# All attention in native float32 products on halves of the array, and another order for the first two chunks

## The chip, the cores and the metric

The kernel runs on one core of one Trainium2 chip. The metric is the device time of one execution in microseconds (us). Before the change the median of three runs is 740.6 us (740.05, 740.6, 743.92).

## The reference

Attention with a local window and a few global columns, and behind it a two-layer network with a GELU, all in float32:

```python
scores = q @ k.T / sqrt(64) - slope[h] * dist          # dist = i - j, or n_local for far global columns
scores = where(is_global | is_local, scores, -1e9)     # n_global = 8 columns, n_local = 96 rows back
a = exp(scores - max) / (sum + 1e-9)
x = a @ v                                              # 4 batches, 8 heads, 768 tokens, 64 per head
h = x.reshape(3072, 512) @ w_in                        # 512 -> 2048
out = gelu(h) @ w_out                                  # 2048 -> 512
```

The weights arrive as float64 words and are turned into float32 on the chip.

## The kernel before, in words

**Tiles.** The 3072 tokens are cut into 12 chunks of 256 (three per batch); a chunk is two blocks of 128 queries. Each block looks at 256 columns: its own 128, the 96 before them and the 32 that hold the global ones (the first block of a batch needs 128). The eight heads of a chunk form four pairs. The network is cut into 8 slices of 256 hidden units. A step `t` is one (chunk, slice), 96 in all: `m1` (line 480) makes `h` with 24 products of 256 columns, `gelu` (495) turns it into `gh + gl`, `m2` (506) adds 12 products of 512 columns to the accumulators `acc`. x, the weights and g are each held as a float32r part and a remainder ("hi" and "lo"), so that three float32r products stand for one of full precision.

**Attention before.** Chunks 0 and 1 (`NATIVE`) multiply plain float32: `scores_pair` (314) puts the two heads of a pair on rows 0-63 and 64-127 of the array, `av_pair` (459) puts them on columns 0-63 and 64-127. The profile shows every such product as two instructions. All other chunks use `split_qk`, `split_v`, `scores` (345), `av_mm` (424): q, k, v and the flipped probabilities are cut into hi and lo by GpSimd, VectorE and ScalarE, and each head then takes whole-array float32r products, 4 per head for the scores (`s`, line 367), 4 for the values (`av`, line 443; 3 in the first chunk of a batch). In both forms VectorE adds the bias and takes the minimum (`n`, `mn`), ScalarE makes the exponentials, GpSimd normalises `n` (line 398), PE transposes it (`t`, line 411) and ScalarE copies it out (`pt`).

**Weights.** Words of a slice come in four pieces of 512 KB (`w`, line 156) through four buffers; `split_weights` (167) decodes a piece: ScalarE the low word, VectorE three operations, ScalarE hi, VectorE lo (lines 180 to 195). Slice s is decoded at step `DECODE[s]` = -6, -4, ..., 8.

**Order.** `run` (561) walks T from -11 to 95 and records m1 of step T+1, m2 of step T and whatever attention falls due: chunk c starts at `START[c]`, and `EV`/`EVN` give the offsets of its parts. `STEPS` starts with slices 0 and 1 of chunk 0, then of chunk 1; from slice 2 on the two chunks take turns. A scheduler then places each engine's instructions by its own estimate of when they become ready; each engine runs its own list in that order. The DMAs of the kernel are issued by SP, q of chunk 0 and the outputs by ScalarE's queue.

Of the kernel before, what the change touches and what calls it, by code (L numbers as in the profile page):

```python
# [17 lines left out]
P = 128  # L18
# [18 lines left out]
EV = {"split": (-1, 0, 3, 4), "v": (3, 4, 7, 8), "s": (0, 1, 4, 5), "exp": (2, 6),  # L37
      "pt": (4, 5, 8, 9), "av": (4, 5, 8, 9)}
EVN = {"split": (-1, 0, 1, 1), "v": (-1, 0, 2, 2), "s": (0, 1, 2, 3), "exp": (0, 1, 3, 3),
       "pt": (2, 3, 4, 5), "av": (2, 3, 4, 5)}  # L40

DECODE = (-6, -4, -2, 0, 2, 4, 6, 8)
LATE = 5

V_POOL = (2,)
NEGMASK = -1000000000.0
WARM_S = False
# [6 lines left out]
def load_scalars(nc, pool, src, name):  # L54
    w = pool.tile([P, 2, 2], I32, name=name + "_w")
    nc.scalar.dma_start(w.rearrange("p i t -> p (i t)"), src.bitcast(I32).partition_broadcast(P))
    f = pool.tile([P, 2, 2], F32, name=name + "_f")
# [12 lines left out]
class Fast:  # L70
    def __init__(self, tc, ctx, qT, kT, v, w, out, limits):
# [10 lines left out]
        self.kq = pool("kq", 2)  # L82
        self.vp = pool("vp", 2)
        self.pp = pool("pp", 4)
# [10 lines left out]
        self.pt_n, self.pt_t, self.av, self.x = {}, {}, {}, {}  # L95
        self.stat, self.g, self.h = {}, {}, {}
        self.acc, self.t3 = {}, {}
        self.last_table = self.last_word = self.last_hi = None

    def consts(self):  # L100
        nc, const = self.nc, self.const
        self.nl, self.ng = load_scalars(nc, const, self.limits, "nn")
        self.ident = const.tile([P, P], F32, name="ident")
        make_identity(nc, self.ident)
        self.pen = const.tile([P, 2 * P], BF16, name="pen")
        self.pen0 = const.tile([P, P], BF16, name="pen0")
        self.kg = const.tile([P, H, 2, NG], F32, name="kg")
        self.nmax = const.tile([P, 8], F32, name="nmax")
        nc.vector.memset(self.nmax, NEGMASK)
        self.qsc = const.tile([P, NP], F32, name="qsc")  # L110
        for p in range(NP):
            for hh in range(2):
                nc.gpsimd.memset(self.qsc[hh * D:(hh + 1) * D, p:p + 1], 1.0 / (8.0 * slope(2 * p + hh)))
        self.wand = const.tile([P, 256], I32, name="wand")
        nc.vector.memset(self.wand, -1)
        ta = self.stg.tile([P, 4, 256], F32, name="ta", tag="stage")
        tb = self.stg.tile([P, 4, 256], F32, name="tb", tag="stage")
        irel, icol = tb[:, 0].bitcast(I32), tb[:, 1, 0:P].bitcast(I32)
        rel, col, keep = ta[:, 0], ta[:, 1, 0:P], ta[:, 2]
        nc.gpsimd.iota(irel, pattern=[[-1, 2 * P]], base=P, channel_multiplier=1)  # L120
        nc.gpsimd.iota(icol, pattern=[[1, P]], base=0, channel_multiplier=0)
        nc.vector.tensor_copy(rel, irel)
        nc.vector.tensor_copy(col, icol)
        nc.vector.tensor_scalar(out=col, in0=col, scalar1=self.ng, scalar2=None, op0=ALU.is_lt)
        nc.vector.tensor_scalar(out=col, in0=col, scalar1=BIG, scalar2=-BIG, op0=ALU.mult, op1=ALU.add)
        nc.vector.tensor_scalar(out=col, in0=col, scalar1=self.nl, scalar2=None, op0=ALU.subtract)
        nc.vector.tensor_scalar(out=keep, in0=rel, scalar1=self.nl, scalar2=None, op0=ALU.is_lt)
        nc.vector.scalar_tensor_tensor(out=keep, in0=rel, scalar=0.0, in1=keep, op0=ALU.is_ge, op1=ALU.mult)
        nc.vector.tensor_scalar(out=keep, in0=keep, scalar1=BIG, scalar2=-BIG, op0=ALU.mult, op1=ALU.add)
        nc.vector.tensor_tensor(out=self.pen, in0=keep, in1=rel, op=ALU.subtract)  # L130
# [3 lines left out]
    def after(self, ins, prev, why):  # L134
        self.tc.add_manual_dep(
            ins, prev.name, mybir.DependencyInfo(mybir.DependencyClass.NoSync, mybir.DependencyReason.DATA),
            reason=why)

# [11 lines left out]
    def lo_dve(self, out, in_, hi):  # L150
        self.nc.vector.tensor_tensor(out=out, in0=in_, in1=hi.bitcast(F32), op=ALU.subtract)  # L151

    def load_words(self, s, i, use):
# [3 lines left out]
        if use == "w":  # L157
            if self.last_word is not None:
                self.after(ins, self.last_word, "weights in order")
            self.last_word = ins  # L160
        return w

    def load_weights(self, s):
        for i in range(4):
            self.raw[s, i, "w"] = self.load_words(s, i, "w")

    def split_weights(self, s):
        nc = self.nc
        if s == LATE:
            self.early.close()  # L170
            self.wts = self.ctx.enter_context(self.tc.tile_pool(name="wlate", bufs=1, side="right"))
        if s == NST - 1:
            self.words.close()
            self.wts = self.ctx.enter_context(self.tc.tile_pool(name="wlast", bufs=1))
        for nm, dst, shape in (("win", self.win, [P, 4, 256]), ("wout", self.wout, [P, 2, 512])):
            dst[s] = tuple(self.wts.tile(shape, F32R, name=f"{nm}{k}{s}") for k in "hl")
        for i in range(4):
            w = self.raw.pop((s, i, "w"))
            lw, hw = w[:, :, 0], w[:, :, 1]
            ins = nc.scalar.activation(out=lw, in_=lw.bitcast(U32), func=AF.Copy, scale=2.0 ** -29).ins  # L180
            if self.last_hi is not None:
                self.after(ins, self.last_hi, "a piece begins when ScalarE is through with the one before")
            a = self.sm.tile([P, 512], I32, name=f"wb{s}_{i}", tag="o")
            nc.vector.tensor_scalar(out=a, in0=hw, scalar1=0x07FFFFFF, scalar2=3,
                                    op0=ALU.bitwise_and, op1=ALU.logical_shift_left)
            nc.vector.scalar_tensor_tensor(out=a, in0=hw, scalar=-0x40000000, in1=a,
                                           op0=ALU.bitwise_and, op1=ALU.bitwise_or)
            nc.vector.tensor_tensor(out=a, in0=a, in1=lw, op=ALU.add)  # L188
            af = a.bitcast(F32)
            if i < 2:  # L190
                hi, lo = (x[:, 2 * i:2 * i + 2, :].rearrange("p d f -> p (d f)") for x in self.win[s])
            else:
                hi, lo = (x[:, i - 2, :] for x in self.wout[s])
            self.last_hi = nc.scalar.copy(hi, af).ins
            self.lo_dve(lo, af, hi)
# [4 lines left out]
    def check_words(self, n):  # L200
# [3 lines left out]
        for e in range(2):  # L204
            nc.vector.scalar_tensor_tensor(out=self.wand, in0=w[:, e * 256:(e + 1) * 256, 1], scalar=0x40000000,
                                           in1=self.wand, op0=ALU.bitwise_xor, op1=ALU.bitwise_and)

    def load_glob(self, b):
        self.kgr = self.stg.tile([P, H, NG], F32, name=f"kgr{b}", tag="stage", padded_shape=[P, H, 128])
        for u in range(2):  # L210
            self.nc.sync.dma_start(self.kgr[u * D:(u + 1) * D], dap(self.kT, b * H * D * S, [[S, D], [D * S, H], [1, NG]]))

    def split_glob(self):
        self.hi_pool(self.kg[:, :, 0, :].bitcast(F32R), self.kgr)
        self.nc.vector.tensor_tensor(out=self.kg[:, :, 1, :], in0=self.kgr, in1=self.kg[:, :, 0, :], op=ALU.subtract)

    def load_qk(self, c, p):
        nc = self.nc
        b, cc = divmod(c, CPB)
        k0 = (b * H + 2 * p) * D * S  # L220
        first = cc == 0
        nb = 1 if first else 2
        if c in NATIVE:
            kr = self.es.tile([P, nb, 256], F32, name=f"kr{c}_{p}", tag="kn", bufs=4)
            qr = self.es.tile([P, CT], F32, name=f"qr{c}_{p}", tag="qn", bufs=4)
            if first:
                nc.sync.dma_start(kr[:, 0, :], dap(self.kT, k0, [[S, P], [1, 256]]))
            else:
                nc.sync.dma_start(kr[:, :, NG:256], dap(self.kT, k0 + cc * CT - 96, [[S, P], [P, 2], [1, 224]]))
                nc.sync.dma_start(kr[:, :, 0:NG], dap(self.kT, k0, [[S, P], [0, 2], [1, NG]]))  # L230
            (nc.scalar if c == 0 else nc.sync).dma_start(qr, dap(self.qT, k0 + cc * CT, [[S, P], [1, CT]]))
            self.raw[c, p] = (kr, qr, nb)
            return
        if p == 0 and (cc == 1 or c == len(NATIVE)):
            self.load_glob(b)
# [572 lines left out]
```

## Time and profile before

| | |
|---|---|
| profiled execution, own time | 742.26 us |
| its span in the trace | 740.5 us |
| median of the runs shown | 740.6 us |
| PE busy | 701.2 us (95%) |
| VectorE busy | 500.8 us (68%) |
| ScalarE busy | 355.7 us (48%) |
| GpSimd busy | 324.9 us (44%) |
| DMA | 80.92 MB, mean 109 GB/s |

Matmuls overlap each other, so the time that a product costs the stream is read from the distance of two starts, not from its duration. "Granted clock" is the share of TensorE's full clock in a stretch.

### The profile page before, as it was taken

Reading aid. Unit: us, or ns where it says so; the run is one execution under the profiler, and the core shown is the slowest. Engines: PE = TensorE matmul, PEld = TensorE weight load, DVE = VectorE, ACT = ScalarE, POOL = GpSimd, SP = SyncE. Lnnn points to the kernel's source line nnn. Section 1 sums busy time; section 2 is a strip of 40 time slices with the busy share of each in tenths; the row PEclk is TensorE's granted clock in tenths of the full one; section 3 lists DMA queues with packets and bytes.
Section 4 is the critical chain, followed back from the end, with each engine's and each line's share of the span. In section 5 each row is a group of like instructions: output and inputs, shape, how many; then the busy total and the mean of one; then the engine's idle time right before and its main releaser. Section 6 shows DMA issues by size and latency. Waiting matters only on the chain.

```text
span 740.5 us, 13471 instructions
## 1 busy us (share of the span) xinstructions
PE 701.2 (95%) x4615; PEld 629.6 (85%) x4615; DVE 500.8 (68%) x1310; ACT 355.7 (48%) x906; POOL 324.9 (44%) x604
## 2 busy tenths in 40 slices
PE   4688998899999999999999999999999999999996
PEld 3446997788999999999889999999899999989995
DVE  6888898956856867866757857856658768634210
ACT  3567547356355455355355355354455455452101
POOL 3764135555345455443543554643444644431110
PEclk8558999999999999999999999999999999999999
DMA  8995552315334434334424334235334431100000
GB/s 247 244 242 184 159 168 73 112 52 158 109 94 122 129 104 115 100 93 126 110 94 135 113 109 128 87 101 128 104 104 119 129 111 43 44 15 1 30 1 32
DMA packets 74396, 80.92 MB, mean 109 GB/s; under 512 B 12368, under 2 KB 63056, under 8 KB 74320
## 3 DMA queue, kind: packets, MB, share of 16 engines
q1 hardware_dynamic: 70144, 73.16, 35.4%
q10 hardware_dynamic: 4176, 6.82, 2.6%
q8 instruction: 38, 0.62, 0.4%
q14 instruction: 38, 0.31, 0.1%
HBM read 73.66 MB, written 6.29 MB: 108 GB/s over the span
## 4 chain that ended last, share of the span: by engine, by line
PE 72%; DMA 10%; DVE 7%; ACT 4%; POOL 3%; issue 2%; SPq 1%; ACTq 0%; POOLq 0%; DVEq 0%
PE h L491 29%; PE acc L521 29%; PE av L443 4%; PE s L367 4%; PE t L411 4%; DMA c<-w 3%; POOL n L398 2%; DMA vr<-v 2%; ACT n L387 2%; DMA w<-w 2%; DMA kr<-kT 1%; DMA qr<-qT 1%; DVE wb L188 1%; DVE gl L151 1%; DVE n L372 1%
## 5 line engine op out<-in xcount | busy, mean ns | idle before, releaser
L491 PE MATMUL h<-xh,winh 128*128 128x256 f32 x768 | 219.1, 285 | 0.0
L491 PE MATMUL h<-xl,winh 128*128 128x256 f32 x768 | 218.0, 284 | 0.0
L491 PE MATMUL h<-xh,winl 128*128 128x256 f32 x768 | 216.7, 282 | 0.0
L521 PE MATMUL acc<-wouth,gh 128*128 128x512 f32 x384 | 154.0, 401 | 6.1 <-POOL gh L145 6.1
L521 PE MATMUL acc<-woutl,gh 128*128 128x512 f32 x384 | 151.6, 395 | 0.0
L491 PEld LDWEIGHTS h<-xh,winh 128*128 128x128 f32 x768 | 146.4, 191 | 2.8 <-issue 0.5
L491 PEld LDWEIGHTS h<-xl,winh 128*128 128x128 f32 x768 | 146.4, 191 | 2.0
L491 PEld LDWEIGHTS h<-xh,winl 128*128 128x128 f32 x768 | 146.3, 191 | 0.4
L398 POOL TENSOR_SCALAR n<-n,su 128x256 f32<-128x256 f32 (+1 forms) x192 | 100.9, 545 | 103.9 <-DVE su L392 89.9
L521 PE MATMUL acc<-wouth,gl 128*128 128x512 f32 x384 | 143.7, 397 | 2.0 <-DVE gl L151 2.0
L501 ACT ACTIVATE gr<-h 128x512 f32<-128x512 f32 x96 | 57.5, 599 | 152.6 <-PE h L491 104.2
L151 DVE TENSOR_TENSOR gl<-gr,gh 128x512 fp32r<-128x512 f32 x96 | 68.1, 710 | 91.1 <-POOL gh L145 91.1
L145 POOL TENSOR_SCALAR gh<-gr 128x512 fp32r<-128x512 f32 x96 | 64.1, 668 | 92.7 <-ACT gr L501 92.7
L145 POOL TENSOR_SCALAR vt<-vr 128x256 fp32r<-128x256 f32 (+1 forms) x80 | 34.5, 432 | 144.9 <-PE av L443 63.4
L387 ACT ACTIVATE n<-n,mn 128x256 f32<-128x256 f32 (+1 forms) x192 | 91.7, 480 | 6.2 <-DVE mn L336 6.0
L521 PEld LDWEIGHTS acc<-wouth,gl 128*128 128x128 f32 x384 | 72.6, 189 | 18.6 <-DVE gl L151 3.4
L521 PEld LDWEIGHTS acc<-wouth,gh 128*128 128x128 f32 x384 | 72.6, 189 | 18.4 <-POOL gh L145 7.5
L521 PEld LDWEIGHTS acc<-woutl,gh 128*128 128x128 f32 x384 | 72.7, 189 | 12.5
L411 PE MATMUL t<-ident,n 128*128 128x128 f32 x352 | 60.8, 291 | 18.0 <-POOL n L398 17.5
L450 ACT COPY t<-av 64x256 f32<-64x256 f32 x80 | 29.3, 366 | 98.2 <-PE av L443 94.7
L420 ACT CAST pt<-t 128x512 fp32r<-128x512 f32 (+1 forms) x80 | 44.3, 554 | 64.0 <-PE t L411 59.4
L411 PEld LDWEIGHTS t<-ident,n 128*128 128x128 f32 x352 | 42.4, 148 | 26.2 <-POOL n L398 22.7
(89 smaller groups left out, 1048.7 us busy)
## 6 DMA issues: line engine op xcount, KB each, us to landing
w<-w SPq DMA_DIRECT2D x32, 512.0 KB, 4.4
c<-w SPq DMA_DIRECT2D x32, 512.0 KB, 3.8
kr<-kT SPq DMA_DIRECT2D x112, 112.0 KB, 2.7
qr<-qT SPq DMA_DIRECT2D x84, 128.0 KB, 3.2
vr<-v SPq DMA_DIRECT2D x48, 128.0 KB, 2.3
out<-o ACTq DMA_DIRECT2D x24, 256.0 KB, 2.3
kr<-kT SPq DMA_DIRECT2D x28, 128.0 KB, 2.7
vr<-v SPq DMA_DIRECT2D x32, 96.0 KB, 2.2
```

Source lines behind the costliest of these rows:

```text
L145: self.nc.gpsimd.tensor_scalar(out=out, in0=in_, scalar1=scale, scalar2=0.0, op0=ALU.mult, op1=ALU.add)
L151: self.nc.vector.tensor_tensor(out=out, in0=in_, in1=hi.bitcast(F32), op=ALU.subtract)
L367: nc.tensor.matmul(sp[:, j, :w], lhsT=qq[:, hh, j * P:(j + 1) * P], rhs=kt[:, t, 0 if first else j, :w], start=t == 0, stop=t == 1)
L387: ins = nc.scalar.activation(out=nn[:, j, :w], in_=nn[:, j, :w], func=AF.Exp, bias=mn[:, i:i + 1], scale=-1.0, accum_out=su[:, i:i + 1])
L398: nc.gpsimd.tensor_scalar(out=nn[:, j, :w], in0=nn[:, j, :w], scalar1=su[:, i:i + 1], scalar2=0.0, op0=ALU.mult, op1=ALU.add)
L411: nc.tensor.transpose(tp[:, i, :], nn[:, j, a * P:(a + 1) * P], self.ident)
L420: nc.scalar.copy(pt[:, :, 0, :], tp[:, :n, :])
L443: nc.tensor.matmul(av[:, j], lhsT=vt[:, vi], rhs=pt[:, i], start=start, stop=stop)
L450: nc.scalar.copy(t1[hr], av[lr, :, 0, :])
L491: nc.tensor.matmul(hp[:, f, :], lhsT=w[:, d, f * P:(f + 1) * P], rhs=x[:, d, :], start=n == 0, stop=n == 3 * NP - 1)
L501: self.table(nc.scalar.activation(out=gr, in_=hp, func=AF.Gelu))
L521: nc.tensor.matmul(acc, lhsT=g[:, f, ks], rhs=w[:, f, :], start=s == 0 and n == 0, stop=s == NST - 1 and n == 5)
```

## The change

Every chunk now uses `scores_pair` and `av_pair`, and the splitting of q, k, v and of the probabilities, the copies of the global columns and the recombination `t1`, `t3` fall away (`split_qk`, `split_v`, `scores`, `av_mm`, `load_glob`, `split_glob`). GpSimd scales q by `qsc` and normalises, nothing else of the attention. A pair's parts follow each other by one step (`EVS`), its exponentials right behind its scores, so there are four batches of exponentials per chunk where there were two. Chunks 0 and 1 are attended first (`EVF`). The steps alternate between chunk 0 and chunk 1 from slice 0 on; two pieces are decoded per step, tied behind the reductions and the exponentials of earlier steps; two pieces may be in ScalarE's and VectorE's hands at a time. Loads of chunk 2 are tied behind slice 1. The constants are built in another order. The cores of the diff:

```diff
-NATIVE = (0, 1)
-START = [-10, -6, 4] + [8 * c - 13 for c in range(3, NCH)]
-STEPS = [(0, 0), (0, 1), (1, 0), (1, 1)] + [(c, s) for s in range(2, NST) for c in range(2)]
+START = [-9, -5] + [8 * c - 12 for c in range(2, NCH)]
+EVF = {"load": (-9, -9, -9, -9), "split": (-1, 0, 1, 2), "s": (0, 1, 2, 3), "pt": (1, 2, 3, 4), "av": (1, 2, 3, 4)}
+EVS = {"load": (-4, -2, 0, 2), "split": (-1, 1, 3, 5), "s": (0, 2, 4, 6), "pt": (1, 3, 5, 7), "av": (2, 4, 6, 8)}
+STEPS = [(c, s) for s in range(NST) for c in range(2)]
...
-DECODE = (-6, -4, -2, 0, 2, 4, 6, 8)
+DECODE = {(0, i): i - 4 for i in range(4)}
+DECODE.update({(s, i): 2 * s - 3 + i // 2 for s in range(1, NST) for i in range(4)})
...
-            if self.last_hi is not None:
-                self.after(ins, self.last_hi, "a piece begins when ScalarE is through with the one before")
+        if len(self.his) > 1:
+            self.after(ins, self.his[-2], "a piece begins when ScalarE is through with the last but one")
+        if self.last_table is not None:
+            self.after(ins, self.last_table, "a piece comes behind the exponentials of earlier steps")
...
+    def load(self, c, p):
...
+        def sync(out, in_):
+            ins = nc.sync.dma_start(out, in_)
+            if c == 2:
+                self.after(ins.ins, self.word_ins[1, 3], "behind the first slices")
+            return ins
...
+    def split(self, c, p):
+        kr, qr, vr = self.raw.pop((c, p))
+        self.hi_pool(qr, qr, self.qsc[:, p:p + 1])
...
-        self.warm(self.bank([P, 512], "warm_ps"), 14)
+        self.warm(self.bank([P, 512], "warm_ps"), 12)
+        self.limit_words = load_words2(self.nc, self.const, self.limits, "nn")
...
+        for p in range(NP):
+            self.load(1, p)
+            self.load_weights(0, p)
+        for s in range(1, NST - 1):
+            for i in range(4):
+                self.load_weights(s, i)
```

How the instructions stand now, at three places. Names carry chunk, head or pair, and a buffer number: s5_0 is the score bank of chunk 5, head 0; qr1_2 is q of chunk 1, pair 2; w1_3 is piece 3 of slice 1; h28 and gh28 belong to step 28.

**PE, between m1 and m2 of a step in the middle** (chunk 5's first scores). Before:

```order
L491 MATMUL h28_3244<-xh3_2196,winl4_928 128x256
L367 MATMUL s5_0_3285<-k5_0_3216,q5_0_3215 128x256 x4
L411 MATMUL t4_5_3293<-ident_129,n4_5_2942 128x128 x4
L521 MATMUL acc3_0_3060<-wouth3_809,gh27_3193 128x512
L521 MATMUL acc3_0_3060<-woutl3_810,gh27_3193 128x512
```

And now:

```order
L352 MATMUL h29_2921<-xh3_1942,winl5_1270 128x256
L270 MATMUL s5_0_2954<-kr5_0_2612,qr5_0_2613 128x256
L270 MATMUL s5_1_2955<-kr5_0_2612,qr5_0_2613 128x256
L270 MATMUL s5_0_2954<-kr5_0_2612,qr5_0_2613 128x256
L270 MATMUL s5_1_2955<-kr5_0_2612,qr5_0_2613 128x256
L382 MATMUL acc3_0_2666<-wouth4_1092,gh28_2883 128x512
```

One head's whole-array products (4 rows in one) have become the half-array products of two heads, enclosed by whole-array products on both sides; the values (`av`) stand likewise between m2 and m1.

**GpSimd, while chunk 0 is attended.** Before, the normalisations of pairs 0 and 1 (heads 0 to 3) followed each other:

```order
L398 TENSOR_SCALAR n0_1_289<-n0_1_289,su0_0_279 128x256
L398 TENSOR_SCALAR n0_2_312<-n0_2_312,su0_1_305 128x128
L398 TENSOR_SCALAR n0_2_312<-n0_2_312,su0_1_305 128x256
L398 TENSOR_SCALAR n0_3_315<-n0_3_315,su0_1_305 128x128
L398 TENSOR_SCALAR n0_3_315<-n0_3_315,su0_1_305 128x256
L145 TENSOR_SCALAR qr1_0_210<-qr1_0_210,qsc_139 128x256
```

And now:

```order
L300 TENSOR_SCALAR n0_1_283<-n0_1_283,su0_0_273 128x256
L146 TENSOR_SCALAR qr1_1_191<-qr1_1_191,qsc_124 128x256
L146 TENSOR_SCALAR qr1_2_202<-qr1_2_202,qsc_124 128x256
L300 TENSOR_SCALAR n0_2_312<-n0_2_312,su0_1_305 128x128
L300 TENSOR_SCALAR n0_2_312<-n0_2_312,su0_1_305 128x256
L300 TENSOR_SCALAR n0_3_315<-n0_3_315,su0_1_305 128x128
L300 TENSOR_SCALAR n0_3_315<-n0_3_315,su0_1_305 128x256
L146 TENSOR_SCALAR qr1_3_213<-qr1_3_213,qsc_124 128x256
```

Pair 1's normalisation now stands behind the scaling of q of chunk 1, pairs 1 and 2, each of which waits for its load.

**GpSimd, where the network begins.** Before:

```order
L398 TENSOR_SCALAR n1_5_610<-n1_5_610,su1_2_600 128x256 x2
L398 TENSOR_SCALAR n1_6_651<-n1_6_651,su1_3_644 128x256 x2
L398 TENSOR_SCALAR n1_7_654<-n1_7_654,su1_3_644 128x256 x2
L145 TENSOR_SCALAR gh0_784<-gr0_786 128x512
L145 TENSOR_SCALAR gh1_864<-gr1_866 128x512
```

And now:

```order
L300 TENSOR_SCALAR n1_7_629<-n1_7_629,su1_3_619 128x256 x2
L146 TENSOR_SCALAR qr2_0_755<-qr2_0_755,qsc_124 128x256
L146 TENSOR_SCALAR gh0_717<-gr0_719 128x512
L146 TENSOR_SCALAR qr2_1_886<-qr2_1_886,qsc_124 128x256
L146 TENSOR_SCALAR qr2_2_1014<-qr2_2_1014,qsc_124 128x256
L146 TENSOR_SCALAR qr2_3_1180<-qr2_3_1180,qsc_124 128x256
L146 TENSOR_SCALAR gh1_788<-gr1_790 128x512
```

The hi part of step 1's g (gh1), which m2 of step 1 multiplies, stands behind the scaling of q of chunk 2, pairs 1 to 3. On SP 22 other loads stand between that of the last piece of slice 1 (w1_3) and that of q of chunk 2, pair 3: all of chunk 2's pairs 0 to 2 (six each) and the four pieces of slice 2.

More of the change, by code (lines that the diff above doesn't have):

```diff
@@ L137, in after, with behind @@
             reason=why)
+    def behind(self, ins):
+        if self.last_dve is not None:
+            self.after(ins.ins, self.last_dve, "behind the reductions of earlier steps")
     def table(self, ins):
@@ L159, in load_words, with load_weights @@
                 self.after(ins, self.last_word, "weights in order")
-            self.last_word = ins
-        return w
[L163 to L167, printed above, removed]
+            self.last_word = self.word_ins[s, i] = ins
+        elif self.last_load is not None:
+            self.after(ins, self.last_load, "behind the loads of earlier steps")
+        return w
+    def load_weights(self, s, i):
+        self.raw[s, i, "w"] = self.load_words(s, i, "w")
@@ L168, in split_weights @@
+    def split_weights(self, s, i):
         nc = self.nc
[L169 to L180, printed above, removed]
-            if self.last_hi is not None:
-                self.after(ins, self.last_hi, "a piece begins when ScalarE is through with the one before")
[L183 to L195, printed above, removed]
+        if i == 0:
+            if s == LATE:
+                self.early.close()
+                self.wts = self.ctx.enter_context(self.tc.tile_pool(name="wlate", bufs=1, side="right"))
+            if s == NST - 1:
+                self.words.close()
+                self.wts = self.ctx.enter_context(self.tc.tile_pool(name="wlast", bufs=1))
+            for nm, dst, shape in (("win", self.win, [P, 4, 256]), ("wout", self.wout, [P, 2, 512])):
+                dst[s] = tuple(self.wts.tile(shape, F32R, name=f"{nm}{k}{s}") for k in "hl")
@@ new lines, in split_weights @@
+        self.behind(nc.vector.tensor_scalar(out=a, in0=hw, scalar1=0x07FFFFFF, scalar2=3,
+                                            op0=ALU.bitwise_and, op1=ALU.logical_shift_left))
+        nc.vector.scalar_tensor_tensor(out=a, in0=hw, scalar=-0x40000000, in1=a,
+                                       op0=ALU.bitwise_and, op1=ALU.bitwise_or)
+        nc.vector.tensor_tensor(out=a, in0=a, in1=lw, op=ALU.add)
+        af = a.bitcast(F32)
+        if i < 2:
+            hi, lo = (x[:, 2 * i:2 * i + 2, :].rearrange("p d f -> p (d f)") for x in self.win[s])
+        else:
+            hi, lo = (x[:, i - 2, :] for x in self.wout[s])
@@ new lines, in load @@
+        two = lambda shape: [2 if c and i == (1 if len(shape) == 3 else 2) else x for i, x in enumerate(shape)]
+        kr = pool.tile([P, nb, 256], F32, name=f"kr{c}_{p}", tag="kn", bufs=bufs, padded_shape=two([P, nb, 256]))
+        qr = pool.tile([P, CT], F32, name=f"qr{c}_{p}", tag="qn", bufs=bufs)
+        vr = pool.tile([P, 2, nb, 2, 64], F32, name=f"vr{c}_{p}", tag="vn", bufs=bufs,
+                       padded_shape=two([P, 2, nb, 2, 64]))
+        ins = (nc.scalar.dma_start if c == 0 else sync)(qr, dap(self.qT, k0 + cc * CT, [[S, P], [1, CT]]))
@@ L391, in exps @@
+        every = [(self.pt_n[c, 2 * p + hh], j, P if first and j == 0 else 256, 2 * hh + j)
+                 for hh in range(2) for j in range(2)]
+        for nn, j, w, i in every:
+            self.table(nc.scalar.activation(out=nn[:, j, :w], in_=nn[:, j, :w], func=AF.Exp, bias=mn[:, i:i + 1],
+                                            scale=-1.0, accum_out=su[:, i:i + 1]))
         nc.vector.tensor_scalar(out=su, in0=su, scalar1=1e-9, scalar2=None, op0=ALU.add)
         nc.vector.reciprocal(out=su, in_=su)
-        for k in range(nb):
-            nn = self.pt_n[c, bt * nb + k]
-            for j in range(2):
-                w = P if first and j == 0 else 256
-                i = 2 * k + j
-                nc.gpsimd.tensor_scalar(out=nn[:, j, :w], in0=nn[:, j, :w], scalar1=su[:, i:i + 1], scalar2=0.0,
-                                        op0=ALU.mult, op1=ALU.add)
+        nc.vector.tensor_tensor(out=self.nmax[:, :4], in0=self.nmax[:, :4], in1=mn, op=ALU.max)
@@ L401, in parts @@
+        for nn, j, w, i in every:
+            nc.gpsimd.tensor_scalar(out=nn[:, j, :w], in0=nn[:, j, :w], scalar1=su[:, i:i + 1], scalar2=0.0,
+                                    op0=ALU.mult, op1=ALU.add)
     def parts(self, c):
@@ new lines, in run @@
+    def run(self, flag_i):
+        wz = self.wz = self.ptp.tile([P, 512], F32R, name="wz", tag="pt", padded_shape=[P, 1024])
+        self.nc.vector.memset(wz.bitcast(F32), 0.0)
+        self.warm(self.bank([P, 512], "warm_ps"), 12)
+        self.limit_words = load_words2(self.nc, self.const, self.limits, "nn")
+        self.load(0, 0)
+        self.consts()
+        for p in range(1, NP):
+            self.load(0, p)
+        for p in range(NP):
+            self.load(1, p)
[3 more added lines that the diff above has]
+                self.load_weights(s, i)
+        last = NCH * NST
```

357 lines of the change are left out of this document (85 added, 272 removed).

## The prediction

> **What bounds the kernel now.** I read the page's row of engines first (PE busy 95%), then the busy time by stages, then the chain of waits through the first stage, and last PE's timeline where half-array products meet whole-array ones. By stages (us; PE, PE's weight loads, DVE, ACT, POOL; granted clock, DMA share, GB/s):
>
> ```profile
> 0.00:10.00 10.00, 7.37 (x30) 5.44 (x30) 5.54 (x28) 1.78 (x3) 4.73 (x20) 1.00 0.76 212
> 10.00:20.00 10.00, 2.89 (x12) 1.62 (x12) 7.28 (x25) 6.37 (x20) 3.44 (x4) 0.67 0.92 265
> 50.00:60.00 10.00, 9.91 (x52) 6.50 (x50) 8.99 (x32) 7.90 (x22) 1.86 (x5) 0.61 0.95 239
> 130.00:140.00 10.00, 10.00 (x58) 8.84 (x57) 9.91 (x24) 4.75 (x12) 5.18 (x8) 0.85 0.29 94
> 200.00:300.00 100.00, 100.00 (x683) 92.57 (x682) 70.96 (x187) 52.65 (x143) 51.49 (x93) 1.00 0.40 112
> 700.00:720.00 20.00, 20.00 (x127) 18.04 (x126) 2.77 (x4) 2.39 (x4) 2.47 (x4) 1.00 0.00 1
> ```
>
> There are two regimes. In the first 60 us DMA moves what it can and PE waits at a lowered clock. Later PE never rests and the clock is full: there only PE's own work counts. 700:720 is the network alone: 127 products in 20 us, 36 in a step, so **a step takes 5.67 us and 96 steps 544.3 us**. The chain of waits through the start:
>
> ```profile
> 48.71 7.22 DMA vr<-v
> ...
> 56.90 3.64 DMA vr<-v
> ...
> 67.74 3.23 PE h L491 x24
> ```
>
> The network's first m1 starts at 67.7, and loads of v, which stand in the queue among chunk 2's k and four slices of words, hold it up.
>
> What attention takes of the saturated stream, from PE's timeline (start, duration):
>
> ```profile
> 604.48 0.28 PE L491 MATMUL h<-xh,winh 128*128 128x256 f32 x1
> 604.60 0.60 PE L411 MATMUL t<-ident,n 128*128 128x128 f32 x4
> 604.95 0.36 PE L491 MATMUL h<-xl,winh 128*128 128x256 f32 x1
> 605.16 0.28 PE L491 MATMUL h<-xh,winl 128*128 128x256 f32 x1
> ...
> 610.02 0.64 PE L443 MATMUL av<-pt,vt 128*128 128x256 f32 x4
> 610.50 0.64 PE L367 MATMUL s<-k,q 128*128 128x256 f32 x4
> 610.98 0.40 PE L521 MATMUL acc<-wouth,gh 128*128 128x512 f32 x1
> ```
>
> Four value or four score products move the next start by 0.48 us, 0.12 each, like an m1 product (604.48 to 604.60). Four transposes take 0.35 and make the m1 product behind them 0.21 instead of 0.12: 0.11 each. The counts for chunks 2 to 11:
>
> ```profile
> L443 PE MATMUL av<-pt,vt 128*128 128x256 f32 x296 | 48.4, 283 | 1.6 <-DVE pt L151 1.6
> L367 PE MATMUL s<-k,q 128*128 128x128 f32 x48 | 8.8, 257 | 0.0
> ```
>
> Values: 296 x 0.12 = 35.5. Scores: 320, of which 48 narrow ones at 0.11 (taken as a transpose), 37.9. Transposes, one per value product: 296 x 0.109 = 32.3. Together **105.7 us**. At the end
>
> ```profile
> 734.06 0.39 PE L521 MATMUL acc<-wouth,gl 128*128 128x512 f32 x1
> ```
>
> is followed by copying and storing, 6.2 us to the span's 740.5. The account: 67.7 + 544.3 + 105.7 + 3.3 (chunk 1's last two value visits and eight transposes, priced as below) + 6.2 = 727.2. That leaves **13.3 us of waits** after the first m1. The profiled execution took 742.3, 1.8 more than its span, and the median of the runs is 740.6, 1.7 less than that execution; so I read a span as a median.
>
> **Term 1: half-array products in the stream.** Both kernels use them in chunks 0 and 1. At full clock the timeline shows
>
> ```profile
> 58.03 1.13 PE L329 MATMUL s<-kr,qr 64*128 64x256 f32 x8
> 59.09 0.88 PE L411 MATMUL t<-ident,n 128*128 128x128 f32 x6
> ...
> 77.89 0.39 PE L521 MATMUL acc<-woutl,gh 128*128 128x512 f32 x1
> 78.21 1.09 PE L474 MATMUL av<-pt,vr 128*64 128x128 f32 x14
> 79.23 0.50 PE L521 MATMUL acc<-wouth,gl 128*128 128x512 f32 x1
> 79.56 0.40 PE L521 MATMUL acc<-wouth,gh 128*128 128x512 f32 x1
> 79.80 0.39 PE L521 MATMUL acc<-woutl,gh 128*128 128x512 f32 x1
> ```
>
> The 8 instructions of a score pair take 1.06 us: the two heads do run side by side. But entering and leaving costs: the product ahead of the values takes 0.32 us where 0.24 is usual (79.56 to 79.80), the one behind them 0.33, together 0.18 more. A score visit is then 1.06 + 0.18 = 1.24 against 8 x 0.12 = 0.96, **+0.28**. The 14 value instructions take 1.02 (here the last two ran without partners, so 16 in pairs need about the same): 1.20 against 0.96, **+0.24**. In a batch's first chunk, scaled by the instructions: scores 1.04 against 0.92, values 1.00 against 0.72, +0.40 a pair. Seven chunks and three, four pairs each: 28 x 0.52 + 12 x 0.40 = **+19.4 us**, so 125.1. A visit between m1 and m2 is not in the trace. Bounds: a visit with entering and leaving hidden (0.30 less for each of 80) gives -5; with half as much again, +31. I take the value between, since it is that of the nearest rows.
>
> The Trainium skill has two rules here. Its page "TensorEngine Tiling (Array Packing)" says under "Theoretical Speedup" that a contraction of up to 64 can gain up to twice; alone that gives the lower bound. Under "Key Properties" it says that changing the tiling mode drains the engine, which speaks against this change and gives the +19.4. The 0.32 and 0.33 us around 78 agree with the second.
>
> **Term 2: the network's start.** Chunk 2's loads and splits and slices 1 to 3 no longer stand ahead of chunk 1. A chain from pair to pair stays: in PE's order a pair's scores stand behind the first transpose of the pair before, which waits for its normalisation. Score starts of before, at half clock, for chunk 0 (first two) and chunk 1:
>
> ```profile
> 17.39 1.65 PE L329 MATMUL s<-kr,qr 64*128 64x128 f32 x8
> ...
> 22.44 1.66 PE L329 MATMUL s<-kr,qr 64*128 64x128 f32 x8
> ...
> 42.27 2.08 PE L329 MATMUL s<-kr,qr 64*128 64x256 f32 x8
> ...
> 48.39 2.07 PE L329 MATMUL s<-kr,qr 64*128 64x256 f32 x4
> ```
>
> So 5.05 us a pair in chunk 0 and 6.1 in chunk 1, with less beside them now. The first scores start when the warm-up ends, near 6.5. But GpSimd's new order puts the scaling of q of chunk 1, pair 2, ahead of pair 1's normalisation. Ahead of that load lie twelve transfers of 128 KB, two pairs of 0.66 MB, two pieces of 0.52 MB and the q itself: 4.06 MB. At 212 GB/s for 10 us and 265 behind, it has landed by 17 to 18; scaling, normalising and transposing put pair 2's scores at 20. Pair 3 follows at 25, chunk 1's pairs at 30, 36, 42 and 48.4. PE's order wants 22 transposes and value products more, some 3.5 us, so **m1 starts at 52**, 15.7 earlier. Bounds: 44 when the q is there in time and chunk 1 goes at 5.05 too; 58 with 8 us a pair in chunk 1, as from 42.27 to 58.03 for two in the old trace.
>
> **Term 3: waits behind it.** At 52 only slice 0 is decoded. VectorE's share of a piece is read off two neighbours:
>
> ```profile
> 73.30 0.68 DVE L186 SCALAR_TENSOR_TENSOR wb<-w,wb 128x512 int32<-128x512 int32 x1
> ...
> 75.56 0.69 DVE L186 SCALAR_TENSOR_TENSOR wb<-w,wb 128x512 int32<-128x512 int32 x1
> ```
>
> 2.26 us with the lo of another piece: 9.0 per slice and 1.2 for two gl, against 11.3 of PE for two steps and more with attention. That fits, but slice 1 does not fit behind chunk 1's last pair: some 2 us at step 2. Cold clock: in 130:140, behind a wait of PE, the clock stood at 0.85 of 10 us, 1.5 us lost; I take 2 for the first m1. Then gh1 stands on GpSimd behind q of chunk 2, pair 3. From the release of slice 0's last buffer (near 54.5) 23 transfers with 4.7 MB precede it; at 250 GB/s they end at 73, gh1 at 74.5. PE wants it 17 us after the first m1 plus the 4 already lost, at 73.4: 1 to 2 us more. With 5 for the later decoding and the middle, where the old kernel lost the 13.3, I take **11 us**; bounds 5 and 20.
>
> What costs nothing: four batches of exponentials per chunk add some 40 table loads to ScalarE, which is busy 53 of 100 us in 200:300. The relief of VectorE and GpSimd there is worth nothing either, as PE is at 100.
>
> **Sum**: 52 + 544.3 + 125.1 + 3.3 + 6.2 + 11 = 741.9, read as a median **742 us**: no change, since under 0.5% (3.7 us) is about what a measurement of this kernel can't tell from none. The early start pays for the visits.
>
> **Rivals.**
> - *The start runs freely* (for it: chunk 1's stages are emptier than in any trace; against: q's place in the queue). m1 at 44, sum 734. Chance 0.25.
> - *Entering and leaving is hidden* between long products, by the page's rule of up to twice: 742 - 24 = 718. Against it: 0.32 and 0.33 beside a 512-column product. 0.07.
> - *GpSimd's queue holds the network up*, the slower side: gh1 waits for q of chunk 2, pair 3, and every transfer ahead of it. It decides as soon as that q lands behind 73; if SP's waits for buffers bring the rate down to 175 GB/s, it lands at 81: 8 us more, 750. 0.22.
> - *Chunk 1 keeps its 8 us a pair*: m1 at 58, 748. 0.13.
> - *The start doesn't move*, since DMA bounds it either way: m1 at 67, 757. 0.04.
>
> **How the numbers follow.** My forecast (738 to 746) has 0.29. From the cases: faster by over 0.5% 0.33, within 0.29, slower 0.38. Eight in ten lie in 727 to 755; the likeliest case's own range is 738 to 746.
>
> **What would show it.** Right: the first m1 between 48 and 56; score and value visits of 1.2 to 1.3 us between m1 and m2; 100 us of the middle holding fewer m1 products than before, some 2.5% longer per chunk; a gap of PE near 70 that q of chunk 2 ends. Wrong: visits under 1.0 us, a first m1 after 60, or PE waiting in the middle for a normalisation, which now has one step of time where it had two.

## The result, and the profile after

| | before | after |
|---|---|---|
| median of the runs | 740.6 us | 750.0 us (746.0 to 750.2) |
| ratio to before, 95% interval | | 1.0106 (1.0068 to 1.0143) |
| profiled execution, own time | 742.26 us | 746.04 us |
| its span | 740.5 us | 744.3 us |
| PE busy | 701.2 us | 715.9 us |
| VectorE, GpSimd busy | 500.8, 324.9 us | 277.0, 182.1 us |

The changed kernel is about 1.1% slower by the ratio; the two medians lie 9.4 us apart. VectorE lost 224 us of work and GpSimd 143, and nothing of it shows in the time. The profiled execution was the quickest of its kernel; the others took 749.4 to 750.2. Where those 4 us lie is the first experiment.

The busy time by stages of the changed kernel (us; PE, PE's weight loads, DVE, ACT, POOL; granted clock, DMA share, GB/s):

```profile
10.00:20.00 10.00, 6.43 (x31) 4.13 (x33) 2.59 (x14) 3.35 (x13) 4.36 (x11) 0.55 0.99 279
30.00:40.00 10.00, 7.09 (x40) 4.54 (x40) 5.04 (x19) 5.49 (x17) 3.81 (x7) 0.75 0.07 10
40.00:50.00 10.00, 6.42 (x33) 4.01 (x34) 4.99 (x17) 4.18 (x12) 3.48 (x6) 0.67 0.30 96
200.00:300.00 100.00, 100.00 (x710) 86.39 (x711) 29.83 (x106) 51.56 (x108) 24.08 (x48) 1.00 0.30 86
```

Before, DMA was the busy one in the start. Now, from 30 to 40, nobody is: DMA 0.07, each engine 38 to 71% busy, and from 10 to 50 the granted clock in these rows is 0.55 to 0.75. That is the mark of one chain of small waits going through all engines. The timeline of PE puts the network's first m1 (before: 67.74) at

```profile
58.03 0.39 PE L352 MATMUL h<-xh,winh 128*128 128x256 f32 x1
```

In the saturated middle, the GELUs count the steps (one instruction of line 362, before of line 501, per step). The same three chunks in both kernels, 24 GELUs, first the changed kernel, then the old one (columns DVE, ACT, POOL busy on that tile; ACT's count is the one to read):

```profile
409.40:582.30 172.90, 16.56 (x24) 14.35 (x24) 14.89 (x24) 1.00 0.30 86
...
411.10:579.50 168.40, 16.60 (x25) 14.38 (x24) 16.43 (x24) 1.00 0.39 112
```

Three chunks take 172.9 us where they took 168.4. The earlier start is paid back at 1.5 us a chunk. In order: the first GELU comes 3.9 us sooner (67.1 against 71.0), the next 16 steps take 112.5 us instead of 116.3, the 72 behind them 513.2 instead of 502.0, the end 0.4 more: 3.8 in sum before rounding, the difference of the two spans.

The price of a visit, from PE's timeline at full clock (start, duration):

```profile
413.55 0.28 PE L352 MATMUL h<-xl,winh 128*128 128x256 f32 x1
413.67 0.28 PE L352 MATMUL h<-xh,winl 128*128 128x256 f32 x1
413.87 1.13 PE L270 MATMUL s<-kr,qr 64*128 64x256 f32 x8
414.94 0.50 PE L382 MATMUL acc<-wouth,gh 128*128 128x512 f32 x1
415.28 0.40 PE L382 MATMUL acc<-woutl,gh 128*128 128x512 f32 x1
...
417.61 0.39 PE L382 MATMUL acc<-wouth,gl 128*128 128x512 f32 x1
417.92 1.09 PE L335 MATMUL av<-pt,vr 128*64 128x128 f32 x16
418.95 0.39 PE L352 MATMUL h<-xh,winh 128*128 128x256 f32 x1
419.17 0.28 PE L352 MATMUL h<-xl,winh 128*128 128x256 f32 x1
```

Read starts. The m1 product ahead of the scores takes 0.20 where its neighbour takes 0.12; the scores take 1.07; the m2 product behind them 0.34 where 0.24 is usual. That is 1.07 + 0.08 + 0.10 = 1.25 us. The values: 0.31 ahead (0.07 over), 1.03, then 0.22 where an m1 product takes 0.12: 1.20. What the 1.07 and the 1.03 are made of is shown with the merged visit below.

Last, the chain of waits through one pair of chunk 1 (start, us, what):

```profile
40.18 1.92 PE s L270 x8
...
42.18 0.23 DVE n L277
...
42.65 0.37 ACT n L294
...
43.06 0.68 ACT n L294 x3
43.74 0.47 ACT pt L317
44.21 0.99 ACT n L294 x4
45.20 0.55 ACT w L182
...
45.81 1.01 POOL n L300
...
46.87 0.69 PE t L313 x2
47.56 2.06 PE s L270 x8
```

From one pair's scores to the next pair's is one closed round: scores 2 us at the low clock, reduction, exponentials 3 us with a copy of the pair before between them, normalisation 1 us, transposes, scores. (The row of `w`, a piece being decoded, stands where VectorE's timeline has the sum's two small operations, 45.23 to 45.62, which the normalisation needs; the decoding itself is not on the round.) The pairs' scores start at 6.9, 11.9, 19.5, 26.1, 32.1, 40.1, 47.5 and 54.3: 5.0 to 8.0 us each.

### The profile page after: what moved, and what is told of

It is laid out like the page before. It is cut to its first block, busy times and chain, and to the rows that moved or that the text cites. A ratio compares the mean times of both kernels' runs of the same rounds, so it can differ in the third digit from the quotient of the medians.

```text
span 744.3 us, 12857 instructions
## 1 busy us (share of the span) xinstructions
PE 715.9 (96%) x4909; PEld 609.8 (82%) x4909; DVE 277.0 (37%) x894; ACT 374.2 (50%) x794; POOL 182.1 (24%) x352
## 4 chain that ended last, share of the span: by engine, by line
PE 80%; DVE 5%; ACT 5%; DMA 4%; issue 3%; POOL 2%; SPq 1%; ACTq 0%; DVEq 0%; POOLq 0%
PE h L352 32%; PE acc L382 32%; PE s L270 6%; PE av L335 5%; PE t L313 4%; ACT n L294 2%; DMA qr<-qT 2%; DVE wb L192 1%; DVE wb L190 1%; POOL n L300 1%; DVE wb L188 1%; SPq L218 1%; DMA w<-w 1%; DMA kr<-kT 1%; ACT w L182 1%
## 5 line engine op out<-in xcount | busy, mean ns | idle before, releaser
L352 PE MATMUL h<-xh,winh 128*128 128x256 f32 x768 | 225.4, 293 | 0.0
L382 PE MATMUL acc<-wouth,gh 128*128 128x512 f32 x384 | 158.3, 412 | 1.7 <-POOL gh L146 1.7
L146 POOL TENSOR_SCALAR gh<-gr 128x512 fp32r<-128x512 f32 x96 | 61.0, 635 | 378.3 <-ACT gr L362 376.9
L382 PE MATMUL acc<-wouth,gl 128*128 128x512 f32 x384 | 149.7, 392 | 0.0
L300 POOL TENSOR_SCALAR n<-n,su 128x256 f32<-128x256 f32 (+1 forms) x192 | 93.3, 504 | 74.3 <-DVE su L297 55.3
L277 DVE CUSTOM_DVE_ANT_0 n<-s,pen 128x256 f32<-128x256 f32 (+1 forms) x192 | 68.6, 398 | 110.0 <-PE s L270 110.0
L317 ACT COPY pt<-t 128x512 f32<-128x512 f32 (+1 forms) x96 | 52.0, 545 | 93.3 <-PE t L313 93.3
L313 PE MATMUL t<-ident,n 128*128 128x128 f32 x352 | 69.5, 287 | 7.7 <-POOL n L300 7.6
L335 PE MATMUL av<-pt,vr 128*64 128x128 f32 x704 | 56.0, 290 | 11.1 <-ACT pt L317 11.1
L335 PEld LDWEIGHTS av<-pt,vr 128*64 128x64 f32 x704 | 41.3, 142 | 30.0 <-ACT pt L317 14.6
```

What stands on the lines that cost most here:

```text
L146: self.nc.gpsimd.tensor_scalar(out=out, in0=in_, scalar1=scale, scalar2=0.0, op0=ALU.mult, op1=ALU.add)
L277: ins = nc.vector.tensor_tensor_reduce(out=nn[:, j, :w], in0=sp[hh][:, j, :w], in1=pen, scale=-slope(2 * p + hh), scalar=3e38, op0=ALU.add ...
L300: nc.gpsimd.tensor_scalar(out=nn[:, j, :w], in0=nn[:, j, :w], scalar1=su[:, i:i + 1], scalar2=0.0, op0=ALU.mult, op1=ALU.add)
L313: nc.tensor.transpose(tp[:, i, :], nn[:, j, a * P:(a + 1) * P], self.ident)
L317: nc.scalar.copy(pt, tp[:, :n, :])
L335: nc.tensor.matmul(av[64 * hh:64 * hh + 64, j, :], lhsT=vt[hh][:, vi, :], rhs=pt[hh][:, i, :], start=(j, a) == js[0], stop=(j, a) == js[-1])
```

## The experiments

All medians below come from 5 to 12 runs of the kernel, beside runs of the kernel before on the same chip (medians 738.6 to 741.8 us). The runs were made on three chips, so kernels of different chips are compared by their ratio to the kernel before; the spans and starts of a trace are of one execution.

**The changed kernel again**, unchanged.

> The changed kernel once more, unchanged. Its profiled execution (746.0 us) was the quickest of five, the others took 749.4 to 750.2. Theory: the 4 us lie in the first stage (the chain from pair to pair at a lowered clock), so that a second profile shows the first m1 at 58 to 62 and the same middle, 58.5 us per eight steps, and the same time between 746 and 750. Rival: the middle itself is slower in the other executions, then eight steps take 58.9 us or more with the first m1 at 58.

749.25 us, ratio 1.0130 (1.0109 to 1.0150). The middle is the same to a tenth (58.5 us for eight steps), the first m1 at 58.59. The 4 us lie behind the first m1: step 4 comes 4.6 us later than in the first profile. Of that, 0.6 is the start. The chain of waits:

```profile
75.19 4.83 DMA qr<-qT
...
80.62 0.63 POOL gh L146
81.25 0.04 issue
81.30 2.08 PE acc L382 x4
```

q of chunk 2 landed at 80.0, two us later than in the first profile (78.0), and held gh1 behind it on GpSimd. From one start on PE to the next it was then 3.35 us instead of 1.94, and the granted clock was 0.50 from 83 to 86 us, where it stayed at 1.00 in the first profile: the four products behind the gap follow each other at 0.43 us, not 0.24. So neither theory names the place: it is neither the chain of pairs nor the middle, but the wait that the prediction had foreseen "near 70", in a longer form.

**q tied behind GpSimd's earlier work.** This takes the waits for q out of GpSimd's order (the core of the edit):

```diff
     def split(self, c, p):
-        self.hi_pool(qr, qr, self.qsc[:, p:p + 1])
+        ins = self.hi_pool(qr, qr, self.qsc[:, p:p + 1])
+        if c:
+            self.after(ins.ins, self.norm[p + 1] if c == 1 else self.last_gh, "...")
```

> Scaling of q tied on GpSimd: for chunk 1 behind normalisations of chunk 0, for chunk 2 on behind the gh before it. Theory (two waits by GpSimd's order): the third pair's scores start near 17.3 instead of 19.5 and everything behind them 2.2 us earlier; the gap of 1.94 us at 77.3 goes: 746 against 750, first m1 near 56. Rival (the start is bound by ScalarE's or DMA's work anyway): the third pair starts earlier but the first m1 stays at 57 to 58; only the gap at 77 goes: 748. Null: another load ends both waits at the same time: 750.

744.07 us, 1.0055 (1.0035 to 1.0074), 5.2 below the unchanged kernel. The first m1 came at 56.91, the third pair's scores at 18.3 instead of 19.5. The gap of PE did not go: 1.73 us were left. GpSimd's timeline shows why:

```profile
77.19 0.62 POOL L146 TENSOR_SCALAR gh<-gr 128x512 fp32r<-128x512 f32 x1 [10.07 <-ACT gr L365]
```

gh1 is now released by the GELU alone, and PE reaches m2 of step 1 directly behind m1 of the same step. That GELU and gh take 1.7 us; the wait for q added 0.2 to it in the first profile and 1.6 in the second. The gain is a little over the theory's 4, but from other places than it said: the start gave 1.7, the gap 1.6, and the remaining 1.9 lie behind it, where the clock had dropped in the second profile of the unchanged kernel and here did not.

**Transposes and values one step later in the first two chunks, alone.**

```diff
-START = [-9, -5] + [8 * c - 12 for c in range(2, NCH)]
-EVF = {... "pt": (1, 2, 3, 4), "av": (1, 2, 3, 4)}
+START = [-10, -6] + [8 * c - 12 for c in range(2, NCH)]
+EVF = {... "pt": (2, 3, 4, 5), "av": (2, 3, 4, 5)}
```

> The step of delay for transposes and values of chunks 0 and 1 alone, without the ties of q on GpSimd. Theory (the two add up): both together took 24 us off, the ties alone 5, so this one 19: 730. Rival (with quicker pairs the loads of q stand in the way more): normalisations of chunk 0 wait for q of chunk 1 and gh1 for q of chunk 2, each for some us more than in the changed kernel: 734 to 738.

**726.21 us, 0.9793 (0.9766 to 0.9820)**: 23 us below the changed kernel and quicker than the kernel before. Both theories fell short of it. PE's timeline:

```profile
24.23 1.14 PE L270 MATMUL s<-kr,qr 64*128 64x256 f32 x8
25.30 0.87 PE L335 MATMUL av<-pt,vr 128*64 128x128 f32 x10
...
26.94 0.66 PE L313 MATMUL t<-ident,n 128*128 128x128 f32 x4
27.52 1.14 PE L270 MATMUL s<-kr,qr 64*128 64x256 f32 x8
...
31.61 1.65 PE L270 MATMUL s<-kr,qr 64*128 64x256 f32 x8
...
40.20 0.39 PE L352 MATMUL h<-xh,winh 128*128 128x256 f32 x1
```

Now a pair's scores are recorded ahead of the transposes of the pair before, so two pairs are under way, and behind the first two they come every 3.3 to 4.9 us (3.3 to 4.1 in chunk 1). PE has few gaps, the granted clock is 0.99 from 20 to 30 where it was 0.59, and the scores take 1.07 instead of 2. m1 starts at 40.2, 18 us earlier.

**Both edits together.**

> As the run before, and in chunks 0 and 1 transposes and values one step later, so that a pair's scores stand on PE ahead of the transposes of the pair before (START one earlier). Theory (the chain scores, reductions, exponentials, normalisation, first transpose, next scores sets the 6.5 to 8 us a pair): the pairs come every 5 to 5.5 us, bounded by ScalarE's 4 us a pair; first m1 at 46 to 50, time 738 to 742. Rival 1 (ScalarE's and GpSimd's queues set the pace): first m1 at 54 to 56, 746 as in the run before. Rival 2 (slice 1 isn't decoded earlier, as its words wait for buffers): first m1 near 48, but PE waits some 8 us behind step 0 or 1, 746.

725.03 us, 0.9801 (0.9778 to 0.9825). The first m1 is at 38.62, and PE's one gap near 57 is 1.49 us. The pairs come every 3.2 to 4.7 us, quicker than the 5 to 5.5 of the theory, whose time is missed by 13 us; rival 1 is out, and slice 1 is in time (rival 2 falls). Beside the quicker pairs the tie of q is worth nothing that can be told: the ratio is 0.9801 with it and 0.9793 without. The two do not add, as both shorten the same chain and, in the run with later transposes alone, gh1 already came ahead of the q that had held it.

**Values directly behind the next scores, chunks 2 to 11.** One merged visit in place of two:

```diff
             self.att(T, "s")
+            if T >= START[2]:
+                self.att(T, "av")
             self.att(T, "pt", 1)
...
                 self.m2(T, 1)
-            self.att(T, "av")
+            if T < START[2]:
+                self.att(T, "av")
```

> In chunks 2 to 11 the values of a pair stand directly behind the scores of the next pair but one, between m1 and m2, so that PE goes to half-array products and back once per pair and not twice. Theory (the price is in entering and leaving: 0.09 us ahead of the scores, 0.09 ahead of the values, 0.10 behind them): one entering and perhaps one leaving fall away, 40 x 0.09 to 0.19 = 3.6 to 7.6 us: 742 to 746 against 750, eight steps with a full chunk at 57.7 to 58.1 instead of 58.5. Rival (the half-array products themselves cost more): no change, 750. Rival 2 (going from row halves to column halves costs as much as leaving and entering): no change, and the product between them shows over 0.4 us.

742.92 us, 1.0039 (1.0018 to 1.0059), 6.3 below the unchanged kernel, eight steps with a full chunk 57.7: the theory holds. The same edit upon the quick start:

> The run with both edits (725.0) and a pair's values directly behind the next scores in chunks 2 to 11. Theory (0.2 us a merged visit, as measured in the slower start: 57.7 where 58.5 stood): 40 x 0.2 = 8 us: 717. Rival (the values, which now are due ahead of m2, meet a ScalarE that has slices to decode): 720 to 725, with waits behind steps 4 to 12.

**718.71 us, 0.9683 (0.9654 to 0.9712)**, the quickest version of this study; without the merged visits the ratio was 0.9801. In both settings the 72 steps behind the 16th take 506.3 us where they took 513.2, 6.9 less. The merged visit, taken apart (a row of several instructions gives the start of the first; each such row is from a short window of its own):

```profile
391.01 0.28 PE L355 MATMUL h<-xl,winh 128*128 128x256 f32 x1
391.13 0.28 PE L355 MATMUL h<-xh,winl 128*128 128x256 f32 x1
391.33 0.49 PE L272 MATMUL s<-kr,qr 64*128 64x256 f32 x2
391.65 0.60 PE L272 MATMUL s<-kr,qr 64*128 64x256 f32 x4
392.09 0.38 PE L272 MATMUL s<-kr,qr 64*128 64x256 f32 x2
392.40 0.33 PE L338 MATMUL av<-pt,vr 128*64 128x128 f32 x2
392.56 0.83 PE L338 MATMUL av<-pt,vr 128*64 128x128 f32 x12
393.21 0.28 PE L338 MATMUL av<-pt,vr 128*64 128x128 f32 x2
393.42 0.50 PE L385 MATMUL acc<-wouth,gh 128*128 128x512 f32 x1
393.76 0.39 PE L385 MATMUL acc<-woutl,gh 128*128 128x512 f32 x1
```

Two half-array instructions start side by side, so count in twos. Of the scores the first two take 0.32 to the next start, the four in the middle 0.22 for each two, the last two 0.31. Of the values the first two take 0.16, the twelve in the middle 0.11 for each two, the last two 0.21. So wherever the form changes, the product ahead and the product behind take longer:

| change of form | product ahead | product behind | price |
|---|---|---|---|
| whole array to row halves | 0.20, not 0.12 | 0.32, not 0.22 | 0.18 |
| row halves to column halves | 0.31, not 0.22 | 0.16, not 0.11 | 0.14 |
| column halves to whole array | 0.21, not 0.11 | 0.34, not 0.24 | 0.20 |

Going from row halves to column halves is thus a change like the others. The scores' 1.07 is the same with the values behind them as with m2 because it holds the price of leaving in both cases. Two visits have four changes (0.70 us, read in the same way in the changed kernel's trace), a merged one has three (0.52); the trace has 2.27 us for a merged visit (391.13 to 393.76, less one usual m1 and one usual m2 product) where two took 2.45. Without any change of form, eight score and sixteen value instructions would take 0.88 us (4 x 0.22) and 0.87 (16/12 of the 0.65 of the middle twelve), 1.75 together, less than the 1.92 of the sixteen whole-array products that they replace: the changes of form are the whole price of the half-array products.

The half-array products differ from those around them in another way too: they multiply plain float32, where m1 and m2 use float32r. That is not the cause. The transposes are plain float32 on the whole array, and among m1's products the product ahead of four of them takes its usual 0.12 (604.48 to 604.60 in the kernel before), the four and the product behind 0.56 (to 605.16), which is 4 x 0.11 + 0.12 with nothing over. In the quick start, where transposes stand ahead of scores and both are plain float32, four take 0.58 (26.94 to 27.52 above) where 4 x 0.11 = 0.44: here only the form changes, and 0.14 is over.

**The same with the values first.**

```diff
+            if T >= START[2]:
+                self.att(T, "av")
             self.att(T, "s")
```

> The same with the values ahead of the scores in the merged visit (m1, values, scores, m2). Theory (entering costs 0.09 whichever form stands first, leaving the scores is free, as their last product takes 0.306 to the next start where 0.313 is usual inside, leaving the values costs 0.10): 0.10 less per pair than in the other order, eight steps with a full chunk at 57.3: 713. Rival (the change from column halves to row halves costs what leaving does): 57.7, 717.

730.18 us, 0.9852 (0.9824 to 0.9879). The visit in its timeline:

```profile
301.99 0.28 PE L355 MATMUL h<-xh,winl 128*128 128x256 f32 x1
302.20 1.09 PE L338 MATMUL av<-pt,vr 128*64 128x128 f32 x16
303.22 1.14 PE L272 MATMUL s<-kr,qr 64*128 64x256 f32 x8
304.29 0.50 PE L385 MATMUL acc<-wouth,gh 128*128 128x512 f32 x1
304.63 0.39 PE L385 MATMUL acc<-woutl,gh 128*128 128x512 f32 x1
```

It takes the same as in the other order: 0.09 over ahead, 1.02, 1.07, 0.10 over behind, 2.28. In the middle eight steps take 57.8, 57.4 and 55.7 (57.7, 57.2 and 55.5 in the other order). So leaving the scores is not free, and the rival has the right number. The theory had misread the last score product: its 0.306 was set beside the 0.313 of the first two, which stand at a change of form themselves; inside it is 0.22. The whole is 11 us slower than the other order, since eight steps from the 8th on take 68.5 us instead of 59.5. There PE's list has two steps' m2 together and transposes that wait for their normalisation (PE waited 6.8 us for them in this run, 3.8 in the other); these waits explain 3 of the 11 us, and why the planner orders it so was not pursued.

**The quick start with the old whole-array products in chunks 2 to 11.** START (one tie more, below), EV, the splits, scores and values of the kernel before, upon the run with both edits; chunk 1's tiles get buffers beside those of chunk 0:

```diff
-START = [-10, -6] + [8 * c - 12 for c in range(2, NCH)]
+START = [-10, -6, 4] + [8 * c - 13 for c in range(3, NCH)]
...
+    def tied(self, *a):
+        self.after(self.hi_pool(*a).ins, self.last_gh, "behind GpSimd's work of earlier steps")
```

> The quick start of the run with both edits (725.0), and chunks 2 to 11 attended with the whole-array float32r products of the kernel before, with its splits and offsets. Theory (in the saturated stream the half-array products are the dearer ones): three chunks take 168.4 us in the middle where they took 172.8, ten chunks 14.7 us less: 710. Rival 1 (splitting chunk 2 collides with decoding the slices on VectorE, GpSimd and ScalarE in the first 130 us): 5 to 10 of it given back, 715 to 720, with PE waiting behind steps 4 to 12. Rival 2 (the middle of before is quick only because its start was late): 725.

814.32 us, 1.0971 (1.0937 to 1.1005): far outside every theory, with PE waiting 27.0 us for gh and 15.2 for gl, all through the middle. The added tie held in all chunks, not in chunk 2 alone, and another one put the loads of the checked words behind those of every chunk. Both were taken back to the first chunks; the first of them:

```diff
-        self.after(self.hi_pool(*a).ins, self.last_gh, "behind GpSimd's work of earlier steps")
+        ins = self.hi_pool(*a).ins
+        if self.T < 11:
+            self.after(ins, self.last_gh, "behind GpSimd's work of earlier steps")
```

> The run with the quick start and the whole-array products again, without two ties that the first version had put on every chunk (the splits of k, q and v behind the gh of earlier steps, the loads of the checked words behind those of the chunks); they now hold for chunk 2 alone. Theory (the ties had put GpSimd's splits and gh in each other's way, which shows as PE waiting for gh; without them the middle goes as in the kernel before): eight steps at 56.2, 57.5 and 54.7 in turn, and 14.7 us less than the 725.0 of the quick start with half-array products: 710; 5 more if splitting chunk 2 meets the decoding. Rival (the early start itself disturbs the middle of the whole-array form, as more slices and checks fall together): the middle stays above 60 us for eight steps and the time above 740.

744.50 us, 1.0078 (1.0050 to 1.0106). The middle is that of the kernel before (56.4, 58.1 and 54.1), so half of the theory holds: the ties had done it. But 710 was not reached: the rival's time (above 740) came, though not its sign, eight steps above 60 us through the middle. The busy time of this run, and below it that of the run with later transposes alone, at the same place:

```profile
100.00:120.00 20.00, 15.50 (x98) 12.76 (x96) 18.53 (x34) 8.90 (x20) 16.71 (x21) 1.00 0.45 119
120.00:140.00 20.00, 14.38 (x75) 12.20 (x74) 18.31 (x38) 7.52 (x14) 9.87 (x16) 0.83 0.48 145
140.00:160.00 20.00, 15.12 (x82) 12.68 (x83) 17.73 (x35) 12.57 (x30) 14.78 (x20) 0.88 0.33 92
...
100.00:120.00 20.00, 19.41 (x135) 16.12 (x134) 16.01 (x39) 16.40 (x31) 7.84 (x12) 1.00 0.59 205
120.00:140.00 20.00, 20.00 (x144) 16.70 (x144) 17.95 (x46) 15.47 (x30) 5.84 (x9) 1.00 0.36 101
140.00:160.00 20.00, 19.94 (x146) 17.27 (x143) 4.43 (x20) 11.39 (x27) 4.97 (x11) 1.00 0.40 109
```

Both start the network near 40 and have their first GELU at 47.4 and 47.7. The 16 steps behind it then take 142.4 us with the old products and 111.9 with the new ones. VectorE (third pair of numbers) is nearly full in both until the slices are decoded; that ends at 140 with the new products, but only near 180 with the old ones (17.2 of 20 from 160 to 180), where VectorE also splits k, q, v and the probabilities. From 105 to 200 PE waits 9.4 us for decoded weights and 5.5 for gh, and the clock falls to 0.83. The whole start is given back. VectorE is not alone in it: from 100 to 160 GpSimd stands still for 9.9 us for loads of v that it splits, ahead of gh in its queue, and this run still has the ties of chunk 2, so the share of each was not separated.

## Why the prediction came out as it did

The number, 742, missed by 8 us, and "no change" was not what came; the range of 727 to 755 held, and slower by over 0.5% had the largest chance. Of the signs named as right, the visits, the longer chunk (2.7%) and the gap that q of chunk 2 ends came; the first m1 between 48 and 56 did not. (The chances of the cases add up to 0.32 faster and 0.39 slower, where 0.33 and 0.38 stand; nothing hangs on it.) Point by point:

- **Term 1, the price of the half-array products, was right in its sum, not in its parts.** Predicted 1.24 us for a score visit and 1.20 for a value visit, measured 1.25 and 1.20. Three chunks grew by 4.5 us, where the term gave 5.8 (two full chunks at 2.08 and one first at 1.6); in the same three chunks of the old kernel PE was idle for 1.55 us, in the new one for none. But "1.06 + 0.18" takes the changes of form too low: about half of their price lies inside the 1.06. Taken apart, the products alone are cheaper than the old ones (1.75 against 1.92 a pair) and the four changes cost 0.70. The merged visits show it, with one change less: 0.18 off each, and 6.9 us off the 72 steps in both settings. The rival that hides the changes (718) is out. The rule of the Trainium skill's page "TensorEngine Tiling (Array Packing)", section "Key Properties", that a change of tiling mode drains the engine, agrees with every change of form in the trace, also that between row halves and column halves: 0.14 to 0.20 us each. The trace shows the time, not that it is a drain.
- **Term 2, the network's start, was wrong by 6 us: the step that failed is the pair's period.** I took 5.05 and 6.1 us a pair from the old kernel's start. Measured were 5.0, 7.6, 6.6 and 6.0 up to chunk 1, then 8.0, 7.4 and 6.8: 2 of the 6 us were lost by chunk 1's first scores, 4 within chunk 1. The 6.1 was also the shortest interval that the old trace has in chunk 1. Its scores there start at 33.94, 42.27, 48.39 (the second half of this pair at 51.87) and 58.03, 8.0 us a pair in the mean; that the emptier stages would bring this down to 6.1 was assumed, not read. "A chain from pair to pair stays" was the mistake: the old kernel transposed two steps behind the scores and started chunk 0 with the scores of pairs 0 and 1 side by side, so parts of two pairs overlapped (its intervals in chunk 1 are long all the same, with every stage fuller). The change moved the transposes to one step behind ("pt" stood at (2, 3, 4, 5) in EVN and stands at (1, 2, 3, 4) in EVF) and made the chain a closed round. Putting that single step back moved the first m1 from 58.6 to 40.2. My rival of 8 us a pair in chunk 1 had the right m1 (58) and nearly the time (748), with a chance of 0.13. The two rows of the old chunk 1 that the prediction does not show:

```profile
33.94 2.08 PE L329 MATMUL s<-kr,qr 64*128 64x256 f32 x8
...
51.87 2.07 PE L329 MATMUL s<-kr,qr 64*128 64x256 f32 x4
```

- **The place of q in GpSimd's queue** was read rightly, its size not. The third pair's scores were forecast at 20 and came at 19.5; but taking q out of the way gave 1.2 us there, the rest of that pair's time is the round itself.
- **Term 3, the waits.** 744.3 less the first m1 at 58.0, the steps (544.3), attention as predicted (125.1), chunk 1's rest (3.3) and the tail (6.2) leaves 7.4 us, for which 11 stood. gh1 did wait for q of chunk 2, landing at 78 and 80 where I had 73 (the first m1 was 6 us late too). The rival that GpSimd's queue adds 8 us (750) has the right number by luck: its 8 us are the late start (6.0) and the span read as a median (5.7), less the waits forecast too long (3.6). Tying q gave 5.2 us, of which 1.7 came from the start.
- **Reading a span as a median** cost the rest. The sum, 741.9, stands 2.4 below the span of 744.3 (the start 6.0 short, the waits 3.6 too long). The old kernel's execution took 1.7 more than its median, the new one's 4 less than its own, because, by the two profiles, it met the wait for q in its short form; so the median is 5.7 above the span where I had read the two as one.
- **"The relief of VectorE and GpSimd is worth nothing"** holds where it was said, from 200 on. It does not hold in the first 16 steps, which the sum did not weigh: with the start pulled forward to 40, the same steps take 30 us less with the new products than with the old ones, as far as the last run, with its ties, shows it. The changed kernel could not show it, since its start was held at 58 by the round of pairs.

So the change has two good parts that need each other, the products that take work off VectorE and GpSimd, and the early start, and a table that throws the early start away. What stays open: whether whole-array products from chunk 4 on, behind half-array ones in chunks 2 and 3, would beat 718.7. With 3.7 us less per three chunks (the mean over the 72 steps) to 4.5, eight chunks would bring 725.0 to 713 to 715, an estimate from the traces of before and after; the buffers of both forms do not fit beside each other as they stand, and it was not tried.

## What to carry to other kernels

Before costing a start by the period of an old one, count how many pieces are under way in each: a table that moves a consumer one step nearer to its producer can turn an overlap into a round trip, and the low clock that comes with the gaps makes the round longer still. An offset that costs nothing in a saturated middle deserves its own value in the start. Relief of an engine that is idle in the middle may be what the start needs: look at each stage's busy row, not at the sum. And to price a change of form on PE, read the starts of single instructions at its edges: the total of a visit hides what the edges cost.

## What the hardware showed that was not expected

- Every change between whole array, row halves and column halves costs 0.14 to 0.20 us at full clock, about half on the last product ahead of it and half on the first behind it. A change from row halves to column halves (0.14) is no exception; what looks like the plain duration of a half-array visit holds half of the price. Plain float32 among float32r on the whole array (the transposes) costs nothing of the kind.
- The granted clock turns a chain of waits into a longer one: a pair's eight score instructions show 1.13 us at clock 1.00 and 1.92 to 2.06 in the stretch from 40 to 50, where the mean was 0.67. How much of the 23 us that two pairs under way gained is the clock, and how much the overlap, was not separated.
